# Batch 0's queries in one piece instead of two halves, with new constants in the order planner (attention followed by a SiLU feed-forward layer, one core)

## The chip, the cores and the metric

The kernel runs on one core of a Trainium2 chip. The metric is the device time of one execution in microseconds (us). Before the change the median of 13 runs is 404.85 us (404.15 to 407.69). TensorE (PE in the profile) multiplies matrices, ScalarE (ACT) evaluates functions such as exp and tanh, VectorE (DVE) does elementwise work and 32x32 transposes, GpSimd (POOL) issues the loads, SyncE (SP) the stores.

## The reference

Softmax attention over 8 batches, 12 heads, 448 tokens, 64 dimensions per head; then its output, 3584 tokens of 768 values, goes through a two-layer feed-forward block with SiLU and no bias.

```python
scores = scale * np.matmul(q, k.transpose(0, 1, 3, 2))
scores = scores - np.max(scores, axis=-1, keepdims=True)
attn = np.exp(scores)
attn = attn / (np.sum(attn, axis=-1, keepdims=True) + 1e-09)
attn_out = np.matmul(attn, v)                        # (8, 12, 448, 64)
x = attn_out.transpose(0, 2, 1, 3).reshape(B * S, H * D)
h = x @ w_in                                         # (3584, 768) @ (768, 2048)
g = h * (1.0 / (1.0 + np.exp(-h)))
return g @ w_out                                     # (3584, 2048) @ (2048, 768)
```

## The kernel before, in words

**Attention.** The heads of a batch are taken in groups of four ("hg", three per batch). A *unit* is one batch, one head group and one range of queries (list `units`, L650). Every batch but the first has one range of all 448 queries, so three units; batch 0 is cut by `PIECES` (L196) into two halves of 224 queries, so six units. Keys are cut into four chunks of up to 128. The first four (batch, head group) pairs are "lone": each has all its own key chunks; from there on two units share the last chunk ("rest").

For a unit the kernel loads K and Q in their natural order as fp16 (L237, L251), turns them with DVE (`turn_k` L304, `turn_q` L315), and then issues *score bursts* on PE (L330). Four heads run side by side in four 32-row groups of the array, so a burst of 8 matmuls over 448 queries makes the scores of one key chunk for four heads, in two PSUM tiles `s` of two heads each. There are two such tiles in all (`bufs=2`). ACT turns each into `E` by one exp over 128x896 (L367). With half the queries a burst takes two key chunks, so one exp has the same 896 columns in both cases. For the first units a burst is split by head pair (`split`, L999), so PE can refill one score tile while ACT reads the other; otherwise a burst waits until both are free.

Then come three *attend* steps (L394) per unit: part 0 multiplies E by ones (the softmax denominators), parts 1 and 2 by V, each 16 matmuls in lone units. DVE takes part 0 through transpose, reciprocal, transpose (`inverse`, L434, L440, L443) and scales parts 1 and 2 by it into `xT` (`norm`, L451). Paired units first add three chunks of E on DVE (L378).

**Feed-forward ("MoE" in the code).** `ffn1` (L465): 16 column blocks f of 128, each six matmuls over the 768 inputs, moving the tokens of one piece: 224 tokens at a time for batch 0, 448 for the others. ACT takes tanh of the PSUM tile (L476), DVE forms the gated value G (L512; the halving needed for SiLU from tanh is folded into `norm`). The second layer multiplies G by `w_out`: batch 0's first 256 tokens directly (`plain`, L570, four groups of 16 matmuls), all others as "quads" of two token tiles by Strassen's scheme with seven products (L556), sums of G and of weights on DVE (L546, L502), and read-outs on ACT and DVE (L579, L615 to L629). Output tiles are stored through SP (L609).

**What sets the order.** No loop order is written out. `Order` (L78) simulates the engines while the program is built: `Op` holds a guessed duration, the operations it depends on and a *bias*; at each step ACT and DVE take the waiting operation with the smallest (ready time + bias), so a lower bias is taken earlier (L135). PE is handled in the main loop (L1195): a score burst goes first when its inputs and PSUM tiles are ready and either the *pace* is due (`PACE`, L194: at most one burst per 3.6 us on average, with a credit of up to 8 us, L1213), or no feed-forward group is ready, or fewer than 14 feed-forward groups are queued (L1210); an attend step goes when ready; otherwise the first ready feed-forward group of the first 24 in the list is taken. `ffn1` groups of a piece are queued when its last `norm` has been planned (`after_x`, L957). Loads stand on POOL's queue in an order written out at L704 to L730, with ring counters for the buffers: three for raw Q (`NRQ`), two for raw K. The emitted program is fixed: each engine runs its list in that order and waits at each step for what it needs.

**Zeros.** Until the first `ffn1` group is planned, every PE wait in the plan is filled with matmuls of zeros (`run_zeros`, L1182, L1186): 47 at the start, then as many as fit a planned wait (L1240). They hold one of the four PSUM banks "m", which attend, `ffn1` and the products share; the bank is given back at the first `ffn1`.

Of the kernel before, what the change touches and what calls it, by code (L numbers as in the profile page):

```python
# [28 lines left out]
def act(n):  # L29
    return n * 0.000833 + 0.065  # L30
# [134 lines left out]
def kernel(  # L165
# [16 lines left out]
    TPP = S // 32  # L182
# [8 lines left out]
    NDC = DM // 128  # L191
    NT = 2 * S // 128
    OH = DM // 2
    PACE = 3.6  # L194
    LONE = NG + 1
    PIECES = ((0, 7), (7, TPP))  # L196
    NE, NXT = 9, 16
    NRQ = 3
    NSG, NOST, NTS = 3, 4, 2
# [574 lines left out]
    def queue_ffn1(b, g0, g1):  # L774
        t0, t1 = 32 * g0, 32 * g1
        for f in range(NFF) if b == 0 else [x for f in range(HF) for x in (f, f + HF)]:

            def run(f=f):
                op = Op("PE", NDC * mm(t1 - t0), lambda: ffn1(b, f, t0, t1), tail=PE_OUT)
                if warm["on"]:  # L780
                    warm["on"] = False
                    m_ring.give(od.now)
                m_ring.take()
                od.on_pe(op, "full")
                th = od.add(
                    Op("ACT", act(t1 - t0), lambda: tanh(b, f, t0, t1), [op], -0.3, tail=0.2, ring=th_ring)
                )
                g = Op(
                    "DVE",
                    (t1 - t0) / 960.0 + 0.13,  # L790
                    lambda: gate(b, f, t0, t1),
                    [th],
                    -2,
                    then=lambda at: (m_ring.give(at), th_ring.give(at)),
                )
                g_op.setdefault((b, f), []).append(od.add(g))
                ffn1_left[b] -= 1

            def deps(f=f):
                made = [(x_op[(b, cc, g0)], cc * mm(t1 - t0)) for cc in range(NDC)] + ld_win[f]  # L800

                u, r = divmod(b, 2)
                for qd in range(NT * B // 4) if u else ():
                    if any(t // NT == u - 1 and (r or t % NT < 4) for t in (2 * qd, 2 * qd + 1)):
                        made += (
                            [plain_op.get(x) for x in ((0, 0), (0, 1), (1, 0), (1, 1))]
                            if qd == 0
                            else [pr_op.get((qd, m)) for m in (3, 4, 6, 7)]
                        )
                return made  # L810

            moe.append((deps, 1, run))
            ffn1_left[b] += 1

    def sums_w(ms):

        for m in ms:
            w_op[m] = [
                od.add(
                    Op(  # L820
                        "DVE",
                        0.9,
                        lambda m=m, f0=f0: combine_w(m, f0, f0 + 4),
                        ld_wout[0] + ld_wout[1] + list(plain_op.values()) * (m in (3, 7)),
                        100,
                    )
                )
                for f0 in (0, 4)
            ]

    def queue_plain(t, j):
        def run():
            op = Op("PE", NFF * mm(OH), lambda: plain(t, j), tail=PE_OUT)
            m_ring.take()
            od.on_pe(op, "full")
            plain_op[(t, j)] = op
            od.add(
                Op(
                    "ACT",
                    act(OH),  # L840
                    lambda: take_plain(t, j),
                    [op],
                    -0.3,
                    then=lambda at: (m_ring.give(at), ost_ring.give(at + STORED)),
                    ring=ost_ring,
                )
            )
            if len(plain_op) == 4:
                sums_w((3, 7))

        def deps():
            if any(len(g_op.get((0, f), ())) < len(PIECES) for f in range(NFF)):
                return [None]
            return ld_wout[j] + [(x, f * mm(OH)) for f in range(NFF) for x in g_op[(0, f)]]

        moe.append((deps, 1, run))
# [37 lines left out]
    def queue_quad(qd):  # L894
        quads.append(qd)
        took = {}

        def read(m, eng, fn, deps, *free):
            busy = act(OH) if eng == "ACT" else OH / 960.0 + 0.13
            bias = -0.3 if eng == "ACT" else -4  # L900
            ring = tmp_ring[m] if m in tmp_ring else ost_ring if m in (2, 5, 6, 7) else None

            def then(at):
                for r in free:
                    r.give(at)
                if ring is ost_ring:
                    ring.give(at + STORED)

            took[m] = od.add(Op(eng, busy, lambda: fn(qd), deps, bias, then=then, ring=ring))

        def queue(m, first):
            def run():
                op = Op("PE", HF * mm(OH), lambda: product(qd, m), tail=PE_OUT)
                if BANK[m] == m:
                    m_ring.take()
                if m in (5, 2, 1):
                    op.then = sg_ring.give
                od.on_pe(op, "full")
                pr_op[(qd, m)] = op
                if m == 3:  # L920
                    read(3, "ACT", take_3, [op])
                elif m == 4:
                    read(4, "DVE", take_4, [op, took[3]])
                elif m == 5:
                    read(5, "ACT", take_5, [op], m_ring)
                elif m == 2:
                    read(2, "ACT", take_2, [op], m_ring)
                elif m == 1:
                    read(1, "DVE", take_1, [op, took[4]])
                    read("less_12", "DVE", less_12, [took[1], took[5]])  # L930
                    read("less_21", "DVE", less_21, [took[1], took[2]])
                elif m == 6:
                    read(6, "DVE", take_6, [op, took["less_21"]], m_ring, tmp_ring[1])
                else:
                    read(7, "DVE", take_7, [op, took["less_12"]], m_ring, tmp_ring[3])

            def deps():
                made = list(w_op.get(m, [None])) + [x for y in first if y for x in [took.get(y)]]
                if m in (3, 4):
                    t = 2 * qd + m - 3  # L940
                    for b in {(128 * t + c) // S for c in (0, 127)}:
                        for f in range(HF):
                            x = g_op.get((b, f + HF * (m - 3)), [None])
                            made += [(y, f * mm(OH)) for y in x]
                    return made + ld_wout[0] + ld_wout[1]
                if m in (1, 6, 7):
                    made += [pr_op.get((qd, x)) for x in ((5, 2) if m == 1 else (1,))]
                x = sg_op.get((qd, m), [None, None])
                return made + [x[0], (x[1], 4 * mm(OH))]

            moe.append((deps, 1 if BANK[m] == m else 0, run))


        for m, first in ((3, ()), (4, (3,)), (5, (3,)), (2, (4,)), (1, ()), (6, ()), (7, (1,))):
            queue(m, first)
# [40 lines left out]
    qk_seq, av_seq = [], []  # L996
    for ns in jobs:
        if len(ns) == 1:
            split = ((0,), (1,)) if ns[0] < 5 else ((0, 1),)  # L999
            for c in range(NCH // per_burst(ns[0])):  # L1000

                qk_seq += [(ns, c, ys) for ys in (split if ns[0] + c else ((0, 1),))]
        else:
            qk_seq += [([n], c, (0, 1)) for n in ns for c in range(NCH - 1)]
            qk_seq.append((ns, 3, (0, 1)))
        av_seq += [(ns, part) for part in range(3)]
# [140 lines left out]
    def after_av(n, part, op, nq):  # L1147
        b, hg, g0, g1 = units[n]
        if part == 0:
            made = []  # L1150
            before = ([op] + inv_op[-1:], [], norm_op[-4:])
            for step, busy in enumerate((nq / 960.0 + 0.15, 0.2, nq / 960.0 + 0.15)):
# [2 lines left out]
                    busy,  # L1155
                    lambda step=step: inverse(n, step),
                    made[-1:] + before[step],
                    4,
                )
                made.append(od.add(r))  # L1160
            made[0].then = m_ring.give
# [2 lines left out]
        else:  # L1164
# [2 lines left out]
                nq / 960.0 + 0.13,  # L1167
                lambda: norm(n, part),
                [op] + rdn_op[n],
                -10,  # L1170
                then=m_ring.give,
            )
            x_op[(b, 2 * hg + part - 1, g0)] = od.add(x)
# [21 lines left out]
    while True:  # L1195
# [4 lines left out]
        if od.free["PE"] <= od.now:  # L1200
# [6 lines left out]
                moe_i, moe_next = moe_ready(0)  # L1207
                soon.append(min([x for x in m_ring.free if x>od.now] or [od.now+0.1]))
            if qk is not None and qk <= od.now and (
                od.now >= pace["next"] or moe_i is None or len(moe) < 14  # L1210
            ):
                u0 = units[qk_seq[0][0][0]]
                pace["next"] = min(max(pace["next"], od.now - 8), od.now) + PACE * len(qk_seq[0][2]) / 2  # L1213
                run_qk()
                od.now, keep = od.free["PE"], od.now
                while (a := av_at()) is not None and a <= od.now:

                    if av_seq[0][0][0] < 9 and (x := qk_at()) is not None and x <= od.now + 0:
                        break
                    run_av()  # L1220
                    od.now = od.free["PE"]
# [57 lines left out]
```

The softmax here doesn't subtract the row's maximum and nothing guards it: scores larger than these inputs give would overflow.

## Time and profile before

| what | value |
|---|---|
| median of 13 runs | 404.85 us |
| profiled execution | 404.53 us, of which 402.8 us is the span from the first instruction to the last |
| PE / DVE / ACT / POOL busy in the span | 97% / 75% / 58% / 23% |
| zeros on PE | 96 matmuls, 47 of them at the start |
| first `ffn1` matmul | 22.20 us |
| last `ffn1` matmul on batch 0 ended | before 59.54 us, when `plain` starts |
| last matmul ended, last store's start | about 398.6 us, then read-out and store to 402.8 us |

A busy PE includes the zeros. In the timeline a line holds several instructions of one kind; the distance between the starts of two lines is the time the first really took, while its own duration also holds the last matmul's way through the array and reaches into the next line.

### The profile page before, as it was taken

The numbers are of one execution on the slowest core, as the hardware profiler recorded it, in microseconds if no ns is written. First come the engines' busy times: TensorE is split into PE (matmuls) and PEld (weight loads), VectorE is DVE, ScalarE is ACT, GpSimd is POOL, SyncE is SP. The second block draws the span as 40 slices with busy tenths as digits, with TensorE's granted clock in tenths as the row PEclk, the third lists the DMA queues.
The fourth block names the chain that finished last, engine by engine and source line by source line (L and its number), as shares of the span: only waits on it lengthen the run. The fifth ranks groups of instructions, "written<-read, shape, count | busy, mean of one in ns | idle before, by whom it ended". The sixth has DMA issues, their size and how long they took to land.

```text
span 402.8 us, 9371 instructions
## 1 busy us (share of the span) xinstructions
PE 391.7 (97%) x3752; PEld 200.3 (50%) x3752; DVE 301.6 (75%) x647; ACT 234.2 (58%) x360; POOL 94.5 (23%) x169
## 2 busy tenths in 40 slices
PE   7998999899999999999999999999999999999995
PEld 6666754344444435543444443444445555555563
DVE  2566577999989489758889869798797865775664
ACT  4777986587762784069585485964967324213410
POOL 7742656414000720054000633550000000000000
PEclk9999999999999999999999999999999999999999
DMA  7999999947013960295402785972001220122013
GB/s 114 201 210 205 160 182 180 154 68 116 2 39 81 152 93 2 65 142 99 62 0 56 125 141 51 87 96 55 0 2 42 60 59 2 35 57 68 2 39 117
DMA packets 43355, 34.43 MB, mean 85 GB/s; under 512 B 16944, under 2 KB 42544, under 8 KB 43312
## 3 DMA queue, kind: packets, MB, share of 16 engines
q0 software_dynamic: 32848, 22.82, 40.7%
q1 hardware_dynamic: 10304, 10.83, 10.3%
q8 instruction: 29, 0.48, 0.5%
q10 hardware_dynamic: 160, 0.20, 0.2%
q14 instruction: 14, 0.11, 0.1%
HBM read 45.61 MB, written 11.01 MB: 141 GB/s over the span
## 4 chain that ended last, share of the span: by engine, by line
PE 89%; DVE 3%; DMA 2%; issue 1%; ACT 1%; POOL 1%; ACTq 0%; DVEq 0%; POOLq 0%
PE h L465 36%; PE p L556 29%; PE a L394 12%; PE s L330 10%; PE o L570 3%; DMA V<-in_v_dram 2%; ACT E L367 1%; DVE xT L451 1%; DVE QT L315 1%; POOL rk L237 0%; POOL rq L251 0%; DVE S L546 0%; DVE KT L304 0%; POOL V L264 0%; DVE sT L434 0%
## 5 line engine op out<-in xcount | busy, mean ns | idle before, releaser
L367 ACT ACTIVATE E<-s 128x896 f16<-128x896 f32 (+1 forms) x172 | 148.7, 914 | 29.5 <-PE s L330 28.3
L465 PE MATMUL h<-xT,w_in_t 128*128 128x448 f16 (+1 forms) x864 | 157.6, 333 | 1.5 <-DVE xT L451 1.1
L465 PEld LDWEIGHTS <-w_in_t 128*128 128x128 f16 x864 | 79.5, 98 | 73.2 <-issue 19.6
L476 ACT ACTIVATE th<-h 128x448 f16<-128x448 f32 (+1 forms) x144 | 71.3, 506 | 63.4 <-PE h L465 52.0
L512 DVE SCALAR_TENSOR_TENSOR G<-th,h 128x448 f16<-128x448 f16 (+2 forms) x144 | 74.8, 532 | 34.1 <-ACT th L476 32.1
L264 POOL DMA_DIRECT2D V<-in_v_dram x88 | 48.6, 568 | 121.5 <-PE a L394 106.2
L330 PE MATMUL s<-QT,KT 32*128 32x448 f16 (+4 forms) x864 | 54.3, 340 | 1.4 <-DVE QT L315 0.9
L556 PEld LDWEIGHTS <-G 128*128 128x128 f16 x384 | 36.7, 98 | 27.8 <-issue 3.9
L394 PE MATMUL a<-E,V 128*32 128x448 f16 (+3 forms) x864 | 40.8, 335 | 1.5 <-DVE xT L451 0.5
L556 PEld LDWEIGHTS <-S 128*128 128x128 f16 x312 | 29.0, 98 | 24.1 <-issue 4.8
L451 DVE SCALAR_TENSOR_TENSOR xT<-a,rdn 128x448 f16<-128x448 f32 (+1 forms) x54 | 28.9, 562 | 13.2 <-PE a L394 12.5
L556 PE MATMUL p<-D,G 128*128 128x384 f16 x208 | 37.8, 327 | 0.0
L556 PE MATMUL p<-w_out_t,S 128*128 128x384 f16 x208 | 37.3, 327 | 0.3 <-DVE S L546 0.3
L556 PE MATMUL p<-w_out_t,G 128*128 128x384 f16 x176 | 31.8, 327 | 0.0
L330 PEld LDWEIGHTS <-KT 32*128 32x128 f16 (+2 forms) x864 | 16.3, 99 | 28.8 <-issue 27.6
L394 PEld LDWEIGHTS <-V 128*32 128x32 f16 (+2 forms) x864 | 18.4, 95 | 24.3 <-issue 16.8
L378 DVE TENSOR_TENSOR T<-T,E 128x1792 f16<-128x1792 f16 x20 | 21.8, 1088 | 10.9 <-ACT E L367 10.9
L378 DVE TENSOR_TENSOR T<-E,E 128x1792 f16<-128x1792 f16 x20 | 21.7, 1085 | 9.7 <-ACT E L367 9.6
L546 DVE TENSOR_TENSOR S<-G 128x512 f16<-128x512 f16 x70 | 26.3, 416 | 0.7 <-PE p L556 0.6
L625 ACT COPY ost<-p 128x384 f32<-128x384 f32 x13 | 6.2, 480 | 29.6 <-DMA out_dram<-ost 15.4
L237 POOL DMA_DIRECT2D rk<-in_k_dram x24 | 13.7, 571 | 40.9 <-DVE KT L304 35.2
L304 DVE STREAM_TRANSPOSE KT<-rk 128x192 f32<-128x192 f32 (+3 forms) x49 | 16.7, 378 | 6.4 <-DMA rk<-in_k_dram 6.4
(42 smaller groups left out, 265.1 us busy)
## 6 DMA issues: line engine op xcount, KB each, us to landing
out_dram<-ost SPq DMA_DIRECT2D x196, 48.0 KB, 1.6
rk<-in_k_dram POOLq DMA_DIRECT2D x24, 224.0 KB, 5.4
rq<-in_q_dram POOLq DMA_DIRECT2D x18, 224.0 KB, 5.8
w_out_t<-in_moe_w_out_dram POOLq DMA_DIRECT2D x8, 384.0 KB, 12.1
V<-in_v_dram POOLq DMA_DIRECT2D x43, 64.0 KB, 3.8
V<-in_v_dram POOLq DMA_DIRECT2D x40, 48.0 KB, 3.6
w_in_t<-in_moe_w_in_dram POOLq DMA_DIRECT2D x6, 256.0 KB, 6.9
w_in_t<-in_moe_w_in_dram POOLq DMA_DIRECT2D x3, 512.0 KB, 12.5
```

Of the source, the lines that this page charges most:

```text
L264: nc.gpsimd.dma_start(out=VT[b].rearrange("p h c i e -> p h c (i e)")[32 * x : 32 * (x + 1), hs, 0:count], in_=v[b, hs].rearrange("h (i g) ...
L304: nc.vector.transpose(out=turned.rearrange("p c x i -> p x c i")[:, x:y, c0 : min(c1, count)], in_=t[:, first : first + count * (y - x)].r ...
L330: nc.tensor.matmul(out=pS[p0 : p0 + 32 * (x1 - x0), h % 2, at : at + nq], lhsT=KT[(b, hg)][32 * h : 32 * (h + 1), c, x0:x1, :, e], rhs=QT[ ...
L367: nc.scalar.activation(out=E[(n, w)][0:kr, 2 * y : 2 * y + 2, 0:nk], in_=pS_t[(n, w, y)][0:kr, :, 0:nk], func=AF.Exp, scale=attn_scale,)
L378: nc.vector.tensor_tensor(out=T_t[n], in0=E[(n, 0)] if c == 1 else T_t[n], in1=E[(n, c)], op=ALU.add,)
L394: nc.tensor.matmul(out=a[32 * h : 32 * (h + 1), 0:nq], lhsT=w, rhs=e[k0:k1, h, at : at + nq], start=start, stop=stop,)
L451: nc.vector.scalar_tensor_tensor(out=xT[(b, cc)][:, 32 * g0 : 32 * g1], in0=acc[(n, part)][:, 0:nq], scalar=0.5, in1=rdn_t[n].rearrange("p ...
L465: nc.tensor.matmul(out=h[:, 0 : t1 - t0], lhsT=w_in_t[:, cc, 128 * f : 128 * (f + 1)], rhs=xT[(b, cc)][:, t0:t1], start=(cc == 0), stop=(c ...
L476: nc.scalar.activation(out=th, in_=h_t[(b, f, t0)][:, 0 : t1 - t0], func=AF.Tanh)
L512: nc.vector.scalar_tensor_tensor(out=dst[:, f, at + lo : at + hi], in0=th_t[(b, f, t0)][:, lo - t0 : hi - t0], scalar=1.0, in1=h_t[(b, f, ...
L546: nc.vector.tensor_tensor(out=dst[:, f0:f1], in0=x[:, f0:f1], in1=y[:, f0:f1], op=op)
L556: nc.tensor.matmul(out=pr_t[(qd, BANK[m])][:, 0:OH], lhsT=w[:, f, :], rhs=W_[m][:, f, :], start=(f == 0 and BANK[m] == m), stop=(f == HF - 1),
```

## The change

Batch 0 gets one range of 448 queries, so three units instead of six, and units are numbered 0 to 23 instead of 0 to 26. The two bounds on unit numbers follow (5 to 3, 9 to 6). With that, per batch 0:

- raw Q is loaded by three transfers of 224 KB instead of six of 112 KB, all six of K and Q ahead of V; the three later ones, which waited for free Q buffers, are gone from between V and `w_in` in POOL's queue;
- turns, inverses, norms, attends, score bursts, `ffn1` groups, tanh and gates act on 448 columns instead of 224, in half as many instructions (exps: as many as before, of the same size);
- `ffn1` of batch 0 can begin only when all three units are normalised.

The other edits are constants of the planner: the pace 3.6 to 3.8 us with a credit of 16 instead of 8 us, and not applied while fewer than 30 (not 14) feed-forward groups are queued; biases of tanh (-0.3 to -1), gate (-2 to -4), weight sums (100 to 30), ACT read-outs (-0.3 to -2), inverse (4 to 2) and norm (-10 to -1).

```diff
-    PACE = 3.6
+    PACE = 3.8
-    PIECES = ((0, 7), (7, TPP))
+    PIECES = ((0, TPP),)
...
                 th = od.add(
-                    Op("ACT", act(t1 - t0), lambda: tanh(b, f, t0, t1), [op], -0.3, tail=0.2, ring=th_ring)
+                    Op("ACT", act(t1 - t0), lambda: tanh(b, f, t0, t1), [op], -1, tail=0.2, ring=th_ring)
...
                     lambda: gate(b, f, t0, t1),
                     [th],
-                    -2,
+                    -4,
...
                         lambda m=m, f0=f0: combine_w(m, f0, f0 + 4),
                         ld_wout[0] + ld_wout[1] + list(plain_op.values()) * (m in (3, 7)),
-                        100,
+                        30,
...
                     lambda: take_plain(t, j),
                     [op],
-                    -0.3,
+                    -2,
...
-            bias = -0.3 if eng == "ACT" else -4
+            bias = -2 if eng == "ACT" else -4
...
-            split = ((0,), (1,)) if ns[0] < 5 else ((0, 1),)
+            split = ((0,), (1,)) if ns[0] < 3 else ((0, 1),)
...
                     lambda step=step: inverse(n, step),
                     made[-1:] + before[step],
-                    4,
+                    2,
...
                 lambda: norm(n, part),
                 [op] + rdn_op[n],
-                -10,
+                -1,
...
-                od.now >= pace["next"] or moe_i is None or len(moe) < 14
+                od.now >= pace["next"] or moe_i is None or len(moe) < 30
...
-                pace["next"] = min(max(pace["next"], od.now - 8), od.now) + PACE * len(qk_seq[0][2]) / 2
+                pace["next"] = min(max(pace["next"], od.now - 16), od.now) + PACE * len(qk_seq[0][2]) / 2
...
-                    if av_seq[0][0][0] < 9 and (x := qk_at()) is not None and x <= od.now + 0:
+                    if av_seq[0][0][0] < 6 and (x := qk_at()) is not None and x <= od.now + 0:
```

## The prediction, made before the changed kernel ran

> **What bounds the kernel now.** I read the page's busy shares and slices first, then busy time by stage, then the timeline of each engine in the first 80 us, then PE's waits.
>
> ```profile
> PE 391.7 (97%) x3752; PEld 200.3 (50%) x3752; DVE 301.6 (75%) x647; ACT 234.2 (58%) x360; POOL 94.5 (23%) x169
> PEclk9999999999999999999999999999999999999999
> ```
>
> ```profile
> 6.10:22.20 16.10, 14.91 (x322) 10.55 (x321) 8.58 (x25) 12.92 (x15) 10.31 (x17) 1.00 1.26 191
> 22.20:38.86 16.66, 15.28 (x288) 11.28 (x290) 10.09 (x29) 12.86 (x21) 6.49 (x11) 1.00 1.18 209
> 38.86:59.54 20.68, 19.92 (x239) 13.76 (x239) 13.61 (x35) 18.02 (x37) 11.37 (x20) 1.00 1.18 171
> 59.54:80.00 20.46, 19.32 (x208) 8.76 (x206) 16.82 (x30) 12.53 (x17) 10.60 (x20) 1.00 1.04 169
> 80.00:130.00 50.00, 49.71 (x452) 22.57 (x451) 46.48 (x107) 32.43 (x48) 6.62 (x13) 1.00 0.37 61
> 130.00:300.00 170.00, 169.74 (x1559) 76.07 (x1552) 136.28 (x277) 109.40 (x162) 44.06 (x79) 1.00 0.48 73
> 300.00:398.60 98.60, 98.60 (x658) 53.22 (x656) 68.03 (x144) 34.76 (x61) 0.00 (x0) 1.00 0.17 45
> ```
>
> The columns are the stretch, its length, busy time of PE, weight load, DVE, ACT and POOL, PE's clock, DMA share and GB/s. From 80 to 398.6 us PE lacks 0.55 us of 318.6: there the end is set by PE's amount of work. Time can be won or lost where PE does zeros or waits, before 80 us, or by waits that the new order brings into the full stretch. DMA is saturated to 47 us (191 to 209 GB/s), but the bytes and nearly their order stay.
>
> In the timeline of PE (start, duration, engine, line, operation) two places count.
>
> ```profile
> 9.51 0.57 PE L330 MATMUL s<-QT,KT 32*128 32x224 f16 x8
> 10.01 0.29 PE L1186 MATMUL z<-zeros 128*128 128x128 f16 x2
> 10.23 0.57 PE L394 MATMUL a<-E,ones 128*32 128x224 f16 x16
> ...
> 36.66 2.21 PE L465 MATMUL h<-xT,w_in_t 128*128 128x224 f16 x18
> 38.80 0.57 PE L330 MATMUL s<-QT,KT 32*128 32x448 f16 x8
> 39.30 2.47 PE L465 MATMUL h<-xT,w_in_t 128*128 128x224 f16 x24
> ```
>
> ```profile
> 76.86 0.93 PE L465 MATMUL h<-xT,w_in_t 128*128 128x448 f16 x4
> 78.75 0.35 PE L465 MATMUL h<-xT,w_in_t 128*128 128x448 f16 x1 [0.95 <-DVE xT L451]
> 79.28 0.35 PE L465 MATMUL h<-xT,w_in_t 128*128 128x448 f16 x1 [0.18 <-DVE xT L451]
> 79.56 0.57 PE L330 MATMUL s<-QT,KT 32*128 32x448 f16 x8
> 80.07 2.44 PE L465 MATMUL h<-xT,w_in_t 128*128 128x448 f16 x12
> ```
>
> First: before 22 us PE only serves exps; feed-forward work starts at 22.20 in the gaps of batch 0's second half. Second: batch 0's feed-forward work runs out before batch 1's attention is normalised; six matmuls that take 1.13 us unhindered stretch from 76.86 to 79.56, a loss of 1.56 us.
>
> **Part 1: when ffn1 of batch 0 can start.** ACT's timeline has exp 1 at 6.71 and five exps in 4.32 us, 0.865 each. Batch 0 needs 24 exps before and after, 20.8 us. Before, they end at 34.92, as ACT shares that time with tanh and waits for bursts. After, nothing else is queued on ACT.
> - Exp 1: Q's first load doubles to 224 KB; the extra 0.115 MB at the 0.14 to 0.2 MB per us of the early slices is 0.6 to 0.8 us, and the turn grows from 0.41 to 0.64. Exp 1 at 7.6 us (7.4 to 7.9).
> - Attends of the first two units: six steps of 16x448, 0.88 to 0.92 us each (47.01 to 47.88 shows one), where 16x224 took 0.40 to 0.50. A split burst takes 0.51 of each 0.865 us exp period, so 0.36 is free and a step can delay the next exp by up to 0.54. Laid out by hand against two score tiles, six steps cost 2.1 us. Bounds: nothing if the order slips them in, 6 x 0.90 = 5.4 if each holds ACT for its whole length. The exp gaps of before (0.31, 1.03, 0.58, 0.56 us) are nearest to the smaller figure per step.
> - Zeros: a real one takes 0.064 us (12 in 0.77). The rhythm of 7.68, 8.54, 9.51 is 0.86 and 0.97 us, a little over ACT's. I take 0.3 us; bounds 0 and 24 x 0.05 = 1.2.
> - Last exp ends at 7.6 + 20.8 + 2.1 + 0.3 = 30.8. From the last exp to the second norm took 2.5 us before (34.92 to 37.42). At 448 columns the ones step adds 0.2, transposes 0.22 and 0.23, reciprocal 0.03, two norms 0.46: 3.6 us. The last of six ffn1 matmuls needs that norm, so the group can start 5 x 0.188 = 0.94 earlier: 2.7 us.
> So ffn1 starts at 33.5 us (bounds 30.6 and 38 from the ends above).
>
> POOL loses three Q issues (8.46, 9.26, 11.02; 0.55 us each and 2.85 us of waits), so w_in is issued earlier, yet DMA is full and its bytes are the same: its last part still lands near 34 us (20.12 plus 13.7), after f = 0 to 7 is fed. V has 344 KB more of Q ahead of it instead of the 224 KB of later Q that ran beside it: about 15.5 to 16 us instead of 14.7. Its first user comes at about 17, so nothing; if that cover is gone, exps slip by up to 1 us.
>
> **Part 2: what is left then.** ffn1 groups of 448 take (3.51 - 2.38) / 6 = 0.188 us per matmul (18 against 12, from 82.95 and 80.07); of 224, (2.41 - 1.25) / 12 = 0.097. Batch 0's ffn1 goes from 192 x 0.097 = 18.6 to 96 x 0.188 = 18.05: 0.5 us won. Before, 126 were left at 38.86: 38.86 + 12.2 = 51.06. After: 33.5 + 18.05 = 51.55. The burst at 38.80 (0.51) is still ahead in the first figure; after, PE waits before 33.5 and may have done it: half, -0.25. Net of parts 1 and 2: **+0.25 us** (bounds -3.2 and +5). The start wastes about as much as now: the exps run alone, with less PE work beside them, but end 4 us earlier.
>
> The Trainium skill, "TensorE: Matmul & The Clock Gate", section "Back-to-back issue gap", gives sustained streams with weight loads 81 ns per matmul at 128 columns and 131 ns at 512. Interpolated, as an estimate, that is 93.5 and 122.7 ns for 224 and 448, and ffn1 of batch 0 would gain 17.95 - 11.8 = 6.2 us; the trace's 97 and 188 ns decide for 0.5.
>
> **Part 3: the stall at 77.6.** Batch 1's bursts ran at 35.26, 38.80, 41.71 and so on, about 3 us apart, in spite of the pace of 3.6 (the credit). The new pace and credit leave that. The first can now follow the last exp of batch 0, at 31.2, 4 us earlier, while ffn1 and plain of batch 0 end at the same time as now. V of batch 1 bounds only the attends of its first head group (53.1). So batch 1's norms come up to 4 us earlier and the 1.56 us go: **-1.5 us**. What is late next is the second quad's sum at 119.3 (0.29). If norm's weaker bias costs the lead the gain is nothing. I leave the waits at 55.1 and 59.0 as they are.
>
> **Part 4: the other constants.** Batch 0 frees DVE of 16 gates, 6 norms and their kin: by 32 x 0.38 - 16 x 0.62, 12 x 0.39 - 6 x 0.61 and turns, 3 to 4 us, all beside PE. The thresholds shift bursts, whose last ends near 310 us; after that PE has 88 us of feed-forward work, so an earlier or later end of attention is covered. Biases change what ACT and DVE do first. DVE is 93% busy from 80 to 130 us, so a norm that no longer goes first could come late at a batch's start; queued behind it are its ffn1 and everything after on PE. Bounds: nothing, to 7 batches x 1.56 = 10.9 us; below nothing, the 0.55 us of waits left. I take 0, the present figure for batches 2 to 7, since other PE work is planned there. Tail: the last 4.2 us are the same steps.
>
> **Sum.** +0.25 - 1.5 = -1.25: 404.53 to 403.28 for the profiled execution, which lies 0.32 below the median of 404.85. So 403.6 us.
>
> **Rivals.**
> - *Slower start.* Attends of 0.90 us hold ACT for their whole length (5.4 instead of 2.1) and zeros cost 1.2: ffn1 starts at 37.7, +4.2, 407.8 us. For it: after the first attend at 10.23 ACT idled although a score tile was free. Against: exps of before ran in fours between gaps. It makes the kernel slower from an ffn1 start of 35.6 on. This is the rival of the other sign: 17 in 100.
> - *Late norms.* DVE's new order puts a stall like that of 77.6 at the start of two or three later batches: 403.6 + 2 x 1.56 = 406.7 up to 408.3. Against it: 0.55 us of waits there today; for it: DVE at 93%. 15 in 100.
> - *It cancels.* The stall at 77.6 stays or moves (for instance behind V or the weight sums, taken earlier now) and the start costs 0.25: 405.1, no change to be told. 18 in 100.
> - *Better start.* Exps without gaps: ffn1 at 31.4, 401.5 us. 10 in 100.
> - The forecast, 402.1 to 404.0: 40 in 100.
>
> About 0.2% (0.81 us) is what the measurement can tell from no change. Faster: forecast and better start, 0.50. Same 0.18, slower 0.32. The range of 8 in 10 takes in most of both slower rivals: 401.2 to 407.6; the forecast's own is 402.1 to 404.0.
>
> **What would show it.** In the profile after: exp 1 near 7.6 and exp 24's end near 30.8 (later than 33 speaks for the slower start); first ffn1 near 33.5, 96 of 448 columns on batch 0; zeros up from 96; no idle time of PE before batch 1's ffn1; 80 to 398 still full. Wrong if PE waits for xT at the starts of batches 2 to 7, or if plain starts more than 1 us later than now.

## The result, and the profile after

The changed kernel takes 402.93 us (median of 12 runs, 402.86 to 403.40); the kernel before, over all its runs by then, 405.06 us. The ratio is 0.9947 (95% interval 0.9936 to 0.9958): 0.5% or 2.1 us faster. 403.6 had been forecast. Ratios and intervals, here and below, leave out single slow executions and are not quotients of the two medians, from which they can differ by up to 0.2%. The profiled executions are 1.59 us apart (404.53 and 402.94), their spans 1.6 (402.8 and 401.2); the other half microsecond is that the profiled execution of before is one of its quick ones, while those of the changed kernel lie close together.

The page's busy times, and then busy time by stage (length, PE, weight load, DVE, ACT, POOL, clock, DMA, GB/s), of the changed kernel:

```profile
PE 394.3 (98%) x3479; PEld 189.0 (47%) x3479; DVE 298.7 (74%) x613; ACT 233.1 (58%) x344; POOL 93.0 (23%) x166
PEclk9999999999999999999999999999999999999999
```

```profile
6.10:22.20 16.10, 15.32 (x182) 6.97 (x181) 6.39 (x13) 13.83 (x16) 8.96 (x14) 1.00 1.24 192
22.20:38.86 16.66, 16.61 (x212) 8.02 (x211) 8.47 (x17) 13.29 (x18) 6.25 (x10) 1.00 1.18 208
38.86:59.54 20.68, 20.66 (x173) 8.62 (x172) 14.08 (x24) 16.47 (x25) 11.66 (x20) 1.00 1.19 170
59.54:80.00 20.46, 20.21 (x211) 9.37 (x211) 18.70 (x32) 12.03 (x18) 12.58 (x23) 1.00 1.11 171
80.00:130.00 50.00, 49.98 (x473) 22.61 (x470) 45.57 (x104) 31.85 (x47) 4.40 (x8) 1.00 0.37 67
130.00:300.00 170.00, 169.74 (x1541) 76.15 (x1540) 138.13 (x281) 110.78 (x164) 44.07 (x79) 1.00 0.48 71
```

PE is busier although it has fewer instructions: 159 zeros instead of 96 fill the longer start. From 38.86 to 80 us hardly any wait is left (0.02 and 0.25 us in the two stages, where there were 0.76 and 1.14). DVE lost only 2.9 us of work, and is still busy 91% of the time from 80 to 130 (93% before).

ACT's timeline at the start, then PE's at the two places that the prediction showed (start, duration, engine, line, operation, idle time before and its releaser):

```profile
7.48 7.96 ACT L367 ACTIVATE E<-s 128x896 f16<-128x896 f32 x9 [5.46 <-PE s L330]
15.90 1.73 ACT L367 ACTIVATE E<-s 128x896 f16<-128x896 f32 x2 [0.46 <-PE s L330]
17.81 1.72 ACT L367 ACTIVATE E<-s 128x896 f16<-128x896 f32 x2 [0.18 <-PE s L330]
19.72 3.57 ACT L367 ACTIVATE E<-s 96x896 f16<-96x896 f32 x4 [0.19 <-PE s L330]
23.74 1.73 ACT L367 ACTIVATE E<-s 128x896 f16<-128x896 f32 x2 [0.46 <-PE s L330]
26.08 4.34 ACT L367 ACTIVATE E<-s 128x896 f16<-128x896 f32 x5 [0.62 <-PE s L330]
```

```profile
30.94 0.57 PE L330 MATMUL s<-QT,KT 32*128 32x448 f16 x8
...
33.52 0.57 PE L330 MATMUL s<-QT,KT 32*128 32x448 f16 x8
34.03 2.44 PE L465 MATMUL h<-xT,w_in_t 128*128 128x448 f16 x12
...
76.59 0.57 PE L330 MATMUL s<-QT,KT 32*128 32x448 f16 x8
77.10 2.44 PE L465 MATMUL h<-xT,w_in_t 128*128 128x448 f16 x12
79.48 0.58 PE L330 MATMUL s<-QT,KT 32*128 32x448 f16 x8
```

The 24 exps of batch 0 (9, 2, 2, 4, 2, 5) run from 7.48 to 30.42 us with gaps of 1.91 us. The first bursts of batch 1 follow at 30.94 and 33.52, ffn1 at 34.03. Batch 1's first ffn1 group starts at 77.10 and no longer stops.

That start is a good place to compare the two programs: in both, PE has by then done all of batch 0, batch 1's attention and the same 14 score bursts. Before it is reached at 76.86, after at 77.10. So the new start costs 0.24 us. It would have cost more, had not a wait in the feed-forward stage of batch 0 gone with the change. This attend of batch 1 waited for a norm in the kernel before; in the changed kernel, at 52.88, it does not wait:

```profile
55.09 0.94 PE L394 MATMUL a<-E,V 128*32 128x448 f16 x16 [0.51 <-DVE xT L451]
```

In the kernel before, the first ffn1 group of batch 1 then took 2.70 us (to 79.56) instead of 1.15 (77.10 to 78.25): 1.55 us won. That is 1.3 of the 1.6 us between the spans. The remaining 0.3 comes later; of what lies there, the wait of 0.29 us for a sum at 119.3 is gone. The group no longer stops because batch 1's last two norms come 4 us earlier, as DVE's timeline has it, before and after:

```profile
78.11 1.11 DVE L451 SCALAR_TENSOR_TENSOR xT<-a,rdn 128x448 f16<-128x448 f32 x2
```

```profile
74.02 1.16 DVE L451 SCALAR_TENSOR_TENSOR xT<-a,rdn 128x448 f16<-128x448 f32 x2 [0.43 <-PE a L394]
```

### The profile page after: what moved, and what is told of

The parts are those of the page before. It is cut to its first block, busy times and chain, and to the rows that moved or that the text cites. A ratio compares the mean times of both kernels' runs of the same rounds, so it can differ in the third digit from the quotient of the medians.

```text
span 401.2 us, 8772 instructions
## 1 busy us (share of the span) xinstructions
PE 394.3 (98%) x3479; PEld 189.0 (47%) x3479; DVE 298.7 (74%) x613; ACT 233.1 (58%) x344; POOL 93.0 (23%) x166
## 4 chain that ended last, share of the span: by engine, by line
PE 96%; DMA 1%; ACT 1%; DVE 0%; issue 0%; POOL 0%; POOLq 0%
PE h L465 37%; PE p L556 30%; PE a L394 12%; PE s L330 12%; PE o L570 3%; PE z L1186 2%; DMA rq<-in_q_dram 1%; ACT E L367 0%; POOL rk L237 0%; DVE QT L315 0%; DVE sT L434 0%; DVE ost L615 0%; ACT th L476 0%; POOLq L1263 0%
## 5 line engine op out<-in xcount | busy, mean ns | idle before, releaser
L465 PE MATMUL h<-xT,w_in_t 128*128 128x448 f16 x768 | 155.5, 353 | 0.3 <-DVE sT L434 0.3
L465 PEld LDWEIGHTS <-w_in_t 128*128 128x128 f16 x768 | 71.0, 98 | 78.3 <-issue 17.4
L476 ACT ACTIVATE th<-h 128x448 f16<-128x448 f32 x128 | 69.8, 546 | 63.2 <-PE h L465 50.8
L512 DVE SCALAR_TENSOR_TENSOR G<-th,h 128x448 f16<-128x448 f16 (+1 forms) x128 | 73.8, 583 | 31.6 <-ACT th L476 29.4
L330 PE MATMUL s<-QT,KT 32*128 32x448 f16 (+2 forms) x768 | 55.3, 363 | 1.4 <-DVE QT L315 1.1
L394 PE MATMUL a<-E,V 128*32 128x448 f16 (+2 forms) x768 | 39.5, 356 | 0.0
L451 DVE SCALAR_TENSOR_TENSOR xT<-a,rdn 128x448 f16<-128x448 f32 x48 | 28.1, 615 | 9.2 <-PE a L394 8.7
L394 PEld LDWEIGHTS <-V 128*32 128x32 f16 (+2 forms) x768 | 16.3, 95 | 23.9 <-issue 15.2
L330 PEld LDWEIGHTS <-KT 32*128 32x128 f16 (+2 forms) x768 | 12.9, 98 | 30.8 <-issue 28.4
L434 DVE STREAM_TRANSPOSE sT<-a 128x448 f32<-128x448 f32 x24 | 15.1, 629 | 11.9 <-PE a L394 11.9
```

Of the source, the lines that this page charges most:

```text
L330: nc.tensor.matmul(out=pS[p0 : p0 + 32 * (x1 - x0), h % 2, at : at + nq], lhsT=KT[(b, hg)][32 * h : 32 * (h + 1), c, x0:x1, :, e], rhs=QT[ ...
L394: nc.tensor.matmul(out=a[32 * h : 32 * (h + 1), 0:nq], lhsT=w, rhs=e[k0:k1, h, at : at + nq], start=start, stop=stop,)
L434: nc.vector.transpose(out=sT_t[n], in_=acc[(n, 0)][:, 0 : 32 * (g1 - g0)].rearrange("p (g i) -> p g i", i=32),)
L451: nc.vector.scalar_tensor_tensor(out=xT[(b, cc)][:, 32 * g0 : 32 * g1], in0=acc[(n, part)][:, 0:nq], scalar=0.5, in1=rdn_t[n].rearrange("p ...
L465: nc.tensor.matmul(out=h[:, 0 : t1 - t0], lhsT=w_in_t[:, cc, 128 * f : 128 * (f + 1)], rhs=xT[(b, cc)][:, t0:t1], start=(cc == 0), stop=(c ...
L476: nc.scalar.activation(out=th, in_=h_t[(b, f, t0)][:, 0 : t1 - t0], func=AF.Tanh)
```

## The experiments

My theory was the *lead*: the gain is the lost stall, and the stall is lost because batch 1's attention starts earlier. All times below are medians; ratios are to the kernel before in the same series.

### The parts of the change

One piece and the two bounds on unit numbers, with the old constants (`piece_only`):

```diff
-    PIECES = ((0, 7), (7, TPP))
+    PIECES = ((0, TPP),)
...
-            split = ((0,), (1,)) if ns[0] < 5 else ((0, 1),)
+            split = ((0,), (1,)) if ns[0] < 3 else ((0, 1),)
...
-                    if av_seq[0][0][0] < 9 and (x := qk_at()) is not None and x <= od.now + 0:
+                    if av_seq[0][0][0] < 6 and (x := qk_at()) is not None and x <= od.now + 0:
```

> Batch 0 in one piece and the two bounds on unit numbers, all other constants as before. Theory (lead): the gain comes from the piece alone; batch 1's bursts start some 4 us earlier, so the 1.56 us stall at the start of batch 1's ffn1 goes whatever the constants: ratio to before 0.995, about 403.0 us, first ffn1 near 34 us, no idle time of PE before batch 1's ffn1. Rival (order): the stall went because the new constants took attends or DVE steps in another order; with the old constants it stays at 1 us or more, ratio 0.999 to 1.001, about 405 us.

Measured: 403.25 us, ratio 0.9956 (0.9944 to 0.9969).

The other edits without these three, on two halves (`consts_only`):

> Two halves as before, all the new planner constants (pace, credit, threshold, biases). Theory (lead): constants are worth nothing; first ffn1 at 22 us, a stall of 1 us or more before batch 1's ffn1, ratio 0.999 to 1.001, about 405 us. Rival (order): the constants remove the stall without the piece: ratio about 0.996, 403.4 us.

Measured: 407.23 us, ratio 1.0050 (1.0035 to 1.0064). Slower, which neither theory had.

One piece with the pace, credit and threshold of the change, and one piece with its biases:

```diff
-    PACE = 3.6
+    PACE = 3.8
...
-                od.now >= pace["next"] or moe_i is None or len(moe) < 14
+                od.now >= pace["next"] or moe_i is None or len(moe) < 30
...
-                pace["next"] = min(max(pace["next"], od.now - 8), od.now) + PACE * len(qk_seq[0][2]) / 2
+                pace["next"] = min(max(pace["next"], od.now - 16), od.now) + PACE * len(qk_seq[0][2]) / 2
```

> One piece with the new pace, credit and threshold, the old biases. Theory (lead): as the full change, ratio 0.995, 403.0 us, within 0.4 us of one piece alone. Rival (order): if the pace constants make the difference, this is 1 us or more better than one piece alone; if the biases do, it has the stall, 404.5 us or more.

Measured: 403.52 us, ratio 0.9958 (0.9946 to 0.9971).

The biases are those of tanh (-0.3 to -1), gate (-2 to -4), weight sums (100 to 30), ACT read-outs (-0.3 to -2), inverse (4 to 2) and norm:

```diff
                 [op] + rdn_op[n],
-                -10,
+                -1,
```

> One piece with the new biases, the old pace, credit and threshold. Theory (lead): as the full change, ratio 0.995, 403.0 us, within 0.4 us of one piece alone. Rival (order): if the biases make the difference, 1 us or more better than one piece alone; if the pace does, 404.5 us or more. Rival (late norms): if norm's weaker bias only works with the new pace, new waits for xT show at the starts of batches 2 to 7, 404 to 408 us.

Measured: 403.41 us, ratio 0.9970 (0.9957 to 0.9983).

PE's timeline of the piece alone shows no stall at batch 1's ffn1:

```profile
76.06 0.57 PE L330 MATMUL s<-QT,KT 32*128 32x448 f16 x8
76.57 2.44 PE L465 MATMUL h<-xT,w_in_t 128*128 128x448 f16 x12
78.94 0.57 PE L330 MATMUL s<-QT,KT 32*128 32x448 f16 x8
```

So the piece is enough for the gain. What the other constants add to it does not stand out of the noise: the four ratios with one piece lie between 0.9947 and 0.9970, and their intervals overlap, if barely. The profiles differ in one wait: PE's wait for a sum at 119 us, 0.29 us in the kernel before, is 0.77 us with the piece alone and with the biases, and is gone with the pace constants.

On two halves the constants take the stall away too, as the rival had it: batch 1's first burst is at 33.74 instead of 35.26, and its ffn1 starts at 74.92 without a stop, 1.94 us earlier than in the kernel before. But the run loses more than that later. PE's waits there, and the busy time by stage:

```profile
122.43 0.37 PE L330 MATMUL s<-QT,KT 32*128 32x448 f16 x2 [0.82 <-ACT E L367]
123.24 0.57 PE L330 MATMUL s<-QT,KT 32*128 32x448 f16 x6 [0.44 <-ACT E L367]
124.63 0.40 PE L330 MATMUL s<-QT,KT 32*64 32x448 f16 x4 [0.82 <-ACT E L367]
125.44 0.96 PE L330 MATMUL s<-QT,KT 32*64 32x448 f16 x12 [0.41 <-ACT E L367]
```

```profile
120.00:124.00 4.00, 2.45 (x20) 0.70 (x19) 1.90 (x3) 3.04 (x5) 0.00 (x0) 1.00 0.41 100
124.00:128.00 4.00, 2.83 (x32) 0.75 (x31) 2.89 (x7) 3.12 (x4) 0.00 (x0) 0.65 0.11 26
128.00:132.00 4.00, 4.00 (x44) 1.02 (x40) 2.73 (x6) 1.73 (x2) 0.00 (x0) 0.50 0.02 4
```

PE had no feed-forward work from 120.6 us on and waited for exps, at most 0.82 us at a time but four times in a row: 2.49 of the 3.83 us from 121.61 to 125.44. The granted clock (the third number from the end) fell to one half in that time and was back at 1.00 only at 132 us. Two attend steps of 32 matmuls show the price: 2.86 us at half clock from 129.24, 1.56 after it. What ran the work out is taken up below.

### The lead, taken away

The full change, with batch 1's first burst held in the plan:

```diff
-        return max(at, s, e)
+        hold = 35.3 if n == 3 and c == 0 else 0.0
+        return max(at, s, e, hold)
```

> The full change, but the first burst of batch 1 is held in the plan until 35.3 us, where the kernel before had it; nothing else. Theory (lead): batch 1's attention is late again by 3 to 5 us, PE waits 1 us or more around the start of batch 1's ffn1 (76 to 82 us), 404.0 to 404.8 us, about 1.3 us more than the full change. Rival (wide operations): the stall went because batch 0 leaves DVE 3 to 4 us more room; then it stays away, and the time is within 0.4 us of the full change, 402.6 to 403.4.

Measured: 404.37 us, ratio 0.9978 (0.9954 to 1.0002), 1.4 us over the full change's 402.93. PE's timeline:

```profile
36.37 0.57 PE L330 MATMUL s<-QT,KT 32*128 32x448 f16 x8
...
77.55 0.93 PE L465 MATMUL h<-xT,w_in_t 128*128 128x448 f16 x4
79.43 0.35 PE L465 MATMUL h<-xT,w_in_t 128*128 128x448 f16 x1 [0.95 <-DVE xT L451]
79.96 0.35 PE L465 MATMUL h<-xT,w_in_t 128*128 128x448 f16 x1 [0.18 <-DVE xT L451]
80.24 0.57 PE L330 MATMUL s<-QT,KT 32*128 32x448 f16 x8
```

The first burst is 5.4 us later than in the full change (the change had brought it forward by 4.3, from 35.26 to 30.94, so the run takes away a little more than the lead). The stall of the kernel before is back to the hundredth: 0.95 and 0.18 us of idle time, 2.69 us for the group. The spans nearly add up (2.0 of 1.8 us): the group starts 0.45 us later than in the full change, because PE now spends the wait before 34 us on zeros instead of a burst, and takes 1.54 longer; 403.0 against 401.2. The wide operations' relief of DVE is in this kernel too, so by itself it does not remove the stall.

### The start

The full change, without zeros between the first burst and ffn1:

```diff
-        if warm["on"] and od.free["PE"] <= od.now and wait > 0.05 and od.now > 1.0:
+        if warm["on"] and od.now < 7.0 and od.free["PE"] <= od.now and wait > 0.05 and od.now > 1.0:
```

> The full change with zeros only up to the first score burst; the waits after it up to the first ffn1 are left idle. Theory (the start is set by the exps, zeros cost 0.3 us): first ffn1 at 33.5 to 34.0, granted clock stays at 1.00 since no wait is over 1.3 us, 402.5 to 403.0 us. Rival (clock): the share of idle time counts and not the longest wait, as in the run of the constants alone, whose clock fell to half after waits of at most 0.82 us that left PE idle 60% of 4 us; then bursts and attends take up to twice as long between 10 and 34 us, first ffn1 at 36 or later, 405 to 409 us.

Measured: 406.21 us (404.35 to 409.06), ratio 1.0014 (0.9981 to 1.0047). My expectation fell. PE's first bursts and the busy time by stage in its quickest but one execution:

```profile
6.66 0.58 PE L330 MATMUL s<-QT,KT 32*128 32x448 f16 x8 [0.77 <-DVE QT L315]
8.23 6.77 PE L330 MATMUL s<-QT,KT 32*128 32x448 f16 x28 [1.00 <-ACT E L367]
```

```profile
7.00:8.00 1.00, 0.23 (x8) 0.00 (x0) 0.00 (x0) 0.74 (x1) 0.07 (x1) 1.00 1.11 183
8.00:9.00 1.00, 0.77 (x4) 0.11 (x4) 0.00 (x0) 0.99 (x2) 0.00 (x0) 0.66 1.02 183
10.00:15.00 5.00, 4.60 (x24) 1.12 (x27) 2.00 (x4) 4.46 (x6) 3.19 (x6) 0.50 1.39 191
15.00:20.00 5.00, 5.00 (x53) 1.39 (x56) 2.16 (x4) 3.20 (x4) 2.99 (x5) 0.64 1.25 204
20.00:25.00 5.00, 4.31 (x56) 1.38 (x48) 1.03 (x2) 4.49 (x6) 2.56 (x4) 1.00 1.19 209
```

PE idled 1.77 of the 2.34 us from 5.89 to 8.23, no wait being longer than 1.00 us, and the clock fell to one half until past 18 us. In another run a longer wait did nothing by itself. With the piece alone this one stood before the first burst, and the granted clock stayed at 1.00:

```profile
6.88 0.58 PE L330 MATMUL s<-QT,KT 32*128 32x448 f16 x8 [1.42 <-DVE QT L315]
```

So the longest wait alone does not decide; how much idle time in how long a stretch it takes, these runs do not show. Without zeros ffn1 started at 34.93 instead of 34.03 in this execution, and the span is 1.5 us longer (402.7 against 401.2). The slower executions have no profile, but their mean granted clock is lower still (0.975 in the one of 409.06 us, 0.985 here). Taken with what they do to the clock, zeros do not cost 0.3 us; they are worth some 3 us (406.21 against 402.93, in different series). The Trainium skill, "TensorE: Matmul & The Clock Gate", section "Why this matters for your kernels", asks for no idle gap above about 3 us; in these two runs several gaps in a row of at most 1.00 and 0.82 us were enough.

The full change, with batch 0's attend steps planned in four pieces (unit, part, piece), so that a burst can come between them:

```diff
-        av_seq += [(ns, part) for part in range(3)]
+        K = 4 if ns[0] < 3 else 1
+        av_seq += [(ns, part, k, K) for part in range(3) for k in range(K)]
...
-            for c in range(NCH if lone else NCH - 1):
+            for c in range(NCH * k // K, NCH * (k + 1) // K) if lone else range(NCH - 1):
```

> The full change with each attend step of batch 0 planned in four pieces of four matmuls (one key chunk each). Theory (attends hold exps): pieces of 0.22 us fit the 0.36 us that a split burst leaves of an exp; the gaps of ACT between exps (1.9 us in all) go, the last exp of batch 0 ends near 28.8 instead of 30.4, first ffn1 near 32.5 instead of 34.0, and the time falls by up to 1.5 us, to 401.5 to 402.5, if the order behind it is as good. Rival (the gaps are the way from burst to exp): the last exp still ends at 30 or later and the time is 402.7 or more.

Measured: 409.42 us, ratio 1.0098 (1.0064 to 1.0133). ACT's timeline at the start:

```profile
7.81 7.17 ACT L367 ACTIVATE E<-s 128x896 f16<-128x896 f32 x8 [5.79 <-PE s L330]
15.14 14.60 ACT L367 ACTIVATE E<-s 128x896 f16<-128x896 f32 x16 [0.16 <-PE s L330]
```

The gaps do go, but the exps run at 0.912 us each instead of 0.865: a burst takes 0.80 us with one piece behind it and 1.00 with two (bursts at 16.38, 17.18, 18.18). From first exp to last it is 21.93 us instead of 22.94, so half of the gaps was the price of whole attends, not all of it; the last exp ends at 29.74, between theory and rival, and ffn1 starts at 33.29. The loss of 6 us comes later and not at the start: as with the constants on halves, PE runs out of work at 121 us and the clock falls.

```profile
120.00:124.00 4.00, 2.53 (x23) 0.86 (x22) 1.85 (x3) 2.04 (x4) 0.00 (x0) 1.00 0.30 74
124.00:128.00 4.00, 1.72 (x20) 0.63 (x23) 1.30 (x2) 3.28 (x4) 0.00 (x0) 0.80 0.10 25
128.00:132.00 4.00, 3.87 (x44) 0.77 (x36) 3.93 (x10) 2.01 (x3) 0.00 (x0) 0.50 0.00 0
```

In the timeline the first V attend of batch 2's first pair starts at 111.87 us, against 100.08 in the full change. Its step on ones ran at 91.60 already, so its exps had been ready for 20 us. A pair needs two PSUM banks at once, and my reading of the planner was that mostly one bank was free, which the next feed-forward group took; no trace shows that. Meanwhile E tiles run out: no burst starts between 92.41 and 117.81, until the feed-forward list is empty and only attention is left. A rule that keeps banks for this pair tests it:

```diff
-            if wait is not None and wait <= od.now - 1000 and not (av is not None and av <= od.now):
+            if wait is not None and wait <= od.now - 8 and av_seq[0][0][0] == 6 and not (av is not None and av <= od.now):
```

> The attends in four pieces, and one rule more for batch 2's first pair: when its attend has waited 8 us in the plan for two free PSUM banks, feed-forward groups take no new bank until it has them. Theory (banks): the 409.4 us of the pieces come from that pair, whose attend came 12 us later than in the full change because each bank that came free was taken by a feed-forward group, until these ran out and PE waited for exps from 121 us on with the clock at half; with the rule no such stretch, 403 to 405 us, granted clock 1.00 from 100 to 140 us. Rival: the stretch comes from elsewhere (the DVE or the loads of V) and stays, 408 us or more.

Measured: 403.99 us, ratio 0.9987 (0.9965 to 1.0009): 5.4 us faster than without the rule. The pair's first V attend starts at 98.09, and the clock stays up.

```profile
120.00:124.00 4.00, 3.90 (x39) 1.53 (x36) 3.44 (x8) 3.48 (x5) 0.00 (x0) 1.00 0.40 98
124.00:128.00 4.00, 4.00 (x48) 2.04 (x40) 3.78 (x8) 0.00 (x0) 0.00 (x0) 1.00 0.42 104
128.00:132.00 4.00, 3.71 (x56) 1.38 (x48) 3.79 (x9) 0.00 (x0) 1.00 (x2) 1.00 0.39 97
```

That bears out the banks theory for the pieces, which with the rule come to about the full change again (403.56 in the same series), in spite of the earlier start. That the constants on halves ran dry for the same reason is likely from the same picture (there the pair's two V attends start at 104.29 and 112.46, against 100.08 and 103.05 in the full change, and no burst between 91.41 and 115.44), but was not tried.

### Two halves, with V planned later

The kernel before, old constants, with batch 0's attends on V planned 1 us later:

```diff
-                deps += ld_v[units[n][:2]]
+                deps += [(x, -1.0) for x in ld_v[units[n][:2]]] if b_of(n) == 0 else ld_v[units[n][:2]]
```

> The kernel before, with batch 0's attends on V planned 1 us later. Theory (V wait): what makes the runs before scatter (404.3 to 405.8) is the attend at 14.75 us that waits for V for a time that differs from run to run (0.48 us in the profile of before, 0.76 in that of the constants alone) and holds the exps behind it; planned later, PE does not wait there: scatter at most 0.6 us, median 404.2 to 404.7. Rival: the scatter has another source and stays over 1 us; median 404.7 or more, since the attends come later.

Measured: 402.50 us (402.00 to 403.69), ratio 0.9941 (0.9918 to 0.9963). On scatter I was wrong: 1.7 us, not 0.6. The two executions of this kernel that were profiled, 402.01 us here and 402.65 in the last series, lie 0.62 us apart at the first exp already (6.50 and 7.12) and still at batch 1's ffn1 (75.47 and 76.09): what sets them apart comes before the first exp, and what it is stays open. But the median fell by 2.4 us, where I had expected 0.2 to 0.7. ACT's and PE's timelines say why:

```profile
6.50 4.32 ACT L367 ACTIVATE E<-s 128x896 f16<-128x896 f32 x5 [4.49 <-PE s L330]
11.13 12.41 ACT L367 ACTIVATE E<-s 128x896 f16<-128x896 f32 x13 [0.30 <-PE s L330]
```

```profile
33.18 0.57 PE L330 MATMUL s<-QT,KT 32*128 32x448 f16 x8
...
74.96 0.57 PE L330 MATMUL s<-QT,KT 32*128 32x448 f16 x8
75.47 2.44 PE L465 MATMUL h<-xT,w_in_t 128*128 128x448 f16 x12
```

In the kernel before, the attend at 14.75 us stood in PE's list ahead of two bursts and waited 0.48 us for V, and exps had gaps of 1.03, 0.58, 0.56 us behind it. Here bursts come first, 18 exps run with one gap of 0.30, PE idles 0.77 us from 6.10 to 38.86 where it idled 2.57, batch 1's first burst is at 33.18 instead of 35.26, and the stall is gone: with the same 14 bursts done, batch 1's ffn1 starts at 75.47, 1.39 us before the kernel before and 1.63 before the full change (1.01 in the second execution). Part of this is lost again at 125.19, where an attend waits 0.73 us.

A last series put these side by side: the full change, the halves again, and the halves with most of the new constants.

> The full change once more, beside the halves with V planned late, on the same chip: 402.9 to 403.2 us.

> The two halves with the attends on V planned 1 us later, once more. Theory (lead, not pieces): one piece is worth nothing by itself; what counts is when batch 1's attention starts, 33.2 us here against 35.3 before, so this is as fast as the full change or faster, 402.2 to 402.8 us. Rival: the first measurement was a favourable one, and it is 0.4 us or more slower than the full change.

The constants, on top of V planned later, are the weight sums' bias (100 to 30), that of the quads' ACT read-outs (-0.3 to -2), inverse's (4 to 2) and these:

```diff
-    PACE = 3.6
+    PACE = 3.8
...
-                -10,
+                -4,
...
-                od.now >= pace["next"] or moe_i is None or len(moe) < 14
+                od.now >= pace["next"] or moe_i is None or len(moe) < 30
...
-                pace["next"] = min(max(pace["next"], od.now - 8), od.now) + PACE * len(qk_seq[0][2]) / 2
+                pace["next"] = min(max(pace["next"], od.now - 16), od.now) + PACE * len(qk_seq[0][2]) / 2
```

> The same with most of the new constants (pace 3.8, credit 16, threshold 30, norm -4, inverse 2, weight sums 30, read-outs -2). Theory: with the lead given, the constants move little, 401.8 to 402.8 us. Rival: as with the constants alone on the halves, some attend waits long for two banks, PE runs out of feed-forward work between 110 and 135 us and the clock falls, 404 us or more.

| kernel | median, us | runs from to | ratio to before |
|---|---|---|---|
| before | 404.71 | 403.85 to 412.18 | |
| full change | 403.56 | 402.74 to 404.15 | 0.9964 (0.9947 to 0.9982) |
| halves, V later | 402.65 | 402.12 to 403.33 | 0.9935 (0.9908 to 0.9962) |
| halves, V later, constants | 402.08 | 401.41 to 402.76 | 0.9925 (0.9896 to 0.9954) |

The intervals of the ratios overlap, since the kernel before scatters most; taken directly, the runs of the last line lie below those of the full change but for two hundredths of a microsecond (402.76 against 402.74). The medians of the full change and of the halves with V later are 0.9 us apart.

One piece is therefore not needed for the gain. It is one way to get batch 1's attention started earlier, and the halves, freed of their wait for V, are another. My theory that only this start counts is too narrow, though: the full change starts batch 1's attention at 30.94, before the halves (33.18), and is the slower of the two. A lead of 2.1 us was enough to remove the stall; beyond that, the halves win by a start in which PE loses less time.

The last kernel beats both the kernel before and the full change by these runs, six in number: 2.6 us under before, 1.5 under the full change. In its profile the wait of 0.73 us at 125 us is gone. Here the constants do no harm on halves. Whether that is due to the attends on V or to the constants left as they were (the biases of tanh and gate, and norm's at -4 instead of -1) was not tried.

## Why the prediction was right

- **When ffn1 starts.** Predicted 33.5 us, measured 34.03. First exp 7.6, measured 7.48; gaps between exps 2.1, measured 1.91; last exp's end 30.8, measured 30.42. From there the order put one more burst before ffn1 than I had counted for sure, which is the 0.5 us. The term "six steps cost 2.1 us" has the right sum for a reason only half right: smaller pieces took back 1.0 us of it, and the pace of bursts and pieces is the floor for the rest. The lower bound of the start is a slip: the terms add up to 7.4 + 20.8 + 2.7 = 30.9 and not 30.6, and with it the lower bound of the net is about -2.6 and not -3.2. Nothing in the forecast hangs on it.
- **Start and remaining work, +0.25 us.** Measured +0.24 at the start of batch 1's ffn1 with equal work done. That it fits so well is luck: by the prediction's own terms a start at 34.03 with both bursts done makes 34.03 + 18.05 - 51.06 - 0.51 = +0.5. The wait of 0.51 us at 55.1, which the prediction left as it was, went away, which more than makes up the difference; the remaining 0.2 us were not traced.
- **The stall, -1.5 us.** Measured -1.55. The cause given, bursts 4 us earlier, was shown by taking the lead away. Batch 1's last norms end at 75.2 us in the changed kernel and PE needs them at 78; before they ended at 79.2. Less lead would have done: 2.1 us were enough on halves.
- **The wait for a sum at 119 us.** "Late next" in the prediction, and counted as staying. With one piece it went with the pace constants (it is in the two runs without them and not in those with them), about 0.3 us against the kernel before. The halves with V later do not have it either, with the old pace; they wait at 125 us instead.
- **The other constants, 0.** Right with one piece (differences of a few tenths, within the noise) and by luck: the bound for harm, put on late norms, missed the way in which they do harm on halves, where they cost 2.3 us: PE runs out of work and its clock falls. Of waits for xT in later batches, the rival's mark, there is none.
- **Zeros, 0.3 us.** As a delay the term is about right: with five zeros between them, bursts come 0.88 to 0.92 us apart instead of 0.865, and the 24 exps without their gaps take 21.03 us against 20.8. What it left out is the clock, and that makes the sum of the other sign: without zeros some 3 us are lost.
- **The size.** -1.25 predicted, -1.6 between the profiled executions, -2.1 between medians. 0.3 is the sum at 119 us; the last 0.5 is how far the profiled execution of the kernel before lies under its median, which I had put at 0.32 us. The rivals: the slower start would have needed an ffn1 after 35.6 us, the cancelling one a stall that stayed, the better start exps without gaps; none of these happened.

## What to carry to other kernels

Where a matmul engine is full nearly to the end, look for the few places in which it waits and ask which earlier start would cover them; the change that brings this start need not be the one that was meant. An in-order list should not put work that waits for a load ahead of work that feeds another engine: one microsecond of slack on V was worth more here than the whole change. And a planner that hands out banks one at a time can starve whoever needs two: with the pieces, 5.4 us.

## What the runs showed that I had not expected

- The clock of TensorE halves without any long wait: after 2.49 us of idle time in 3.83, and 1.77 in 2.34, with no single wait above 0.82 and 1.00 us, the granted clock went from 1.00 to 0.50 and stayed there for some 7 and 10 us. One wait of 1.42 us by itself left it at 1.00.
- Zero matmuls in such waits are worth more here than they cost: with them the granted clock stays at 1.00 through the start.
- The same constants change nothing that stands out of the noise on one program and lose 2.3 us on its neighbour. That a pair of attend steps starves for a bank there is likely, and not shown.
